# Crossbar transposes in place of TensorE transposes for q, k and the tails of a windowed attention and MLP kernel

## The chip, the cores and the metric

The kernel runs on one core of one Trainium2 chip. The metric is the device time of one execution in microseconds. The kernel before takes 324.83 us (median of 2 runs, 324.63 to 325.03). Engine names in the profile: PE is TensorE's matrix multiply, PEld its weight load, DVE is VectorE, ACT is ScalarE, POOL is GpSimd, SPq is SyncE's queue, from which nearly all DMA transfers of this kernel are issued.

## The reference, cut to what matters

```python
def _attn_ref(q, k, v):                       # each (8, 8, 576, 64): batch, head, position, head_dim
    scores = q @ k.T / sqrt(64)
    mask = (rel >= 0) & (rel < 64)            # rel = query position - key position
    attn = softmax(where(mask, scores, -1e9))
    return attn @ v

def reference(q, k, v, g_ln, w_ch1, w_ch2):
    x = attention, heads side by side: (8, 576, 512)
    xn = (x - mean) / sqrt(var + 1e-6) * g_ln
    return x + relu(xn @ w_ch1) @ w_ch2       # 512 -> 2048 -> 512
```

The inputs q and k are about 0.1 in size, so the scores are close to zero.

## The kernel before

The program works in groups. Group g runs the MLP of batch g (positions 0 to 511) and, between its steps, the attention of batch g+1 and the preparation of q, k and v of batch g+2. Positions 512 to 575 of all batches, the "tails", form a ninth group; tail i holds batches 2i and 2i+1. Each group from the second batch on has 30 slots: 16 first-layer blocks (slots 0 to 15) and 14 steps of the second layer, which uses 7 products in place of 8. `at(i, f, ...)` puts f into slot i. Every engine works through its own list in order (in the changed kernel PE stands idle for 7.17 us behind one wait, with all its later matmuls in the list).

q and k come from memory in float32, GpSimd casts them to float16, TensorE transposes them (the score matmul of this kernel takes them with the 64 elements of the head dimension on the partitions), and ScalarE copies the transposes from the accumulators (PSUM) to working memory (SBUF):

```python
def load_qk(b, half):                         # b >= 2: 4 heads a half, 4 rows to a partition: 1 KB runs
    nc.sync.dma_start(out=t..., in_=src[b, 4*half:4*half+4, 0:SM, :].rearrange("h (p j) d -> p h (j d)", j=4))

def t_main(b, x, half, eng=None):             # x = 0: q, x = 1: k
    for i in range(8):
        nc.tensor.transpose(out=tp[:, i, :], in_=src[:, i], identity=ident16)
    dst = qkT[b][x][:, 2*half:2*half+2, 64*x:64*x+512]
    evac(..., dst.rearrange("c h (p j) -> c h p j", j=j), tp...rearrange("c (h j) p -> c h p j", j=j))

def s_mm(g, j, ...):                          # 16 score matmuls of 64 x 128 keys and 64 queries
    ...
        lhsT = qkT[g][1][rows, hp, 64*w:64*w+128]
        rhs = qkT[g][0][rows, hp, 64*w:64*w+64]
        nc.tensor.matmul(out=sc[par][:, hp, iw, :], lhsT=lhsT, rhs=rhs, ...)
    ...
        nc.scalar.activation(out=pt[:, par], in_=sc[par], func=AF.Exp, bias=0.0, scale=scale)
```

Then VectorE multiplies `pt` by the mask, TensorE multiplies by v into `xps`, and VectorE writes the normalised attention into a tile of `x_norm`. That tile is later the residual input of the MLP, takes its sum, and is what is stored to memory.

```python
p_xn = tc.tile_pool(name="pxn", bufs=4)       # two tiles a batch: batch b+2 takes the tiles of batch b
def b_step(g, kb):
    ...
    nc.vector.tensor_tensor(out=xn, in0=xps[:, :, 0:D], in1=rcp_b, op=ALU.mult)
def store(kb):
    nc.sync.dma_start(out=out[g, 128*kb:128*kb+128, :], in_=x_norm[(g, kb // 2)][:, kb % 2, :])
```

So the store at the end of group g must have landed before the first `b_step` of batch g+2, which stands in slot 2 of the very next group. In the tail's cast the order will matter:

```python
def cast_tail(i):
    nc.gpsimd.memset(vt[:, :, :, D:D+1], 1.0) # vt has one buffer: waits for the tail before
    nc.gpsimd.tensor_copy(out=q16, in_=tq)
    nc.gpsimd.tensor_copy(out=k16, in_=tk)
    nc.gpsimd.tensor_copy(out=vt[:, :, :, 0:D], in_=tv)
```

The softmax here doesn't subtract the row's maximum and nothing guards it: scores larger than these inputs give would overflow.

## Time and profile before

| | kernel before |
|---|---|
| time | 324.83 us |
| profiled span | 322.6 us |
| PE busy | 309.6 us (96%) |
| ACT busy | 176.8 us (55%) |
| PE busy from 103 to 300 us | throughout |

The page of the kernel before: the busy time of each engine (with its share of the span and its number of instructions), then the granted clock of TensorE in 40 slices of the span (in tenths).

```profile
PE 309.6 (96%) x3229; PEld 204.6 (63%) x3229; DVE 204.3 (63%) x388; ACT 176.8 (55%) x292; POOL 164.6 (51%) x251
...
PEclk9999999999999999999999999999999999999998
```

PE is busy nearly all the time at full clock. The matmul time in the profile overlaps (each instruction's end is modelled), so what an instruction costs is read from start to start. The timeline of PE in the kernel before (start in us, duration, engine, line, operation, output and inputs, count), a block of 8 transposes and a block of 16 score matmuls with what follows each:

```profile
117.80 0.62 PE L216 MATMUL tp<-ident,qk 128*128 128x128 f16 x8
118.26 0.93 PE L435 MATMUL pB<-w2s,hrT 128*128 128x256 f16 x7
...
128.88 0.41 PE L263 MATMUL sc<-qkT,qkT 64*128 64x64 f16 x16
129.22 0.40 PE L232 MATMUL tpq<-ident,tq 128*128 128x128 f16 x4
```

Eight transposes take 118.26 - 117.80, about 0.45 us; the score block takes 0.34 us. SyncE's queue in the last part of the same group (the time of issue of each transfer, with the time that the issue took):

```profile
114.06 0.37 SPq L92 DMA_DIRECT2D qk<-in_q_dram  x1
115.05 0.37 SPq L92 DMA_DIRECT2D qk<-in_k_dram  x1
119.20 0.37 SPq L92 DMA_DIRECT2D qk<-in_q_dram  x1
120.19 0.37 SPq L92 DMA_DIRECT2D qk<-in_k_dram  x1
125.07 4.44 SPq L139 DMA_DIRECT2D v<-in_v_dram  x4
129.70 3.70 SPq L401 DMA_DIRECT2D out_dram<-xn  x4
```

The stores of the group are issued from 129.70 us. VectorE needs their tiles back at 135.47 us and waits 0.19 us there. So there is no slack at all, which one sees also in the group of that instruction in the page (after the last bar: idle time of the engine before it, and what ended it):

```profile
L297 DVE TENSOR_TENSOR xn<-xps,rcp 128x512 f32<-128x512 f32 x36 | 24.9, 692 | 3.3 <-DMA out_dram<-xn 2.2
```

The windows of the kernel before, over two stretches (busy time of each engine, then granted clock, busy share of the DMA engines and GB/s; the share can pass 1):

```profile
121.00:127.00 6.00, 6.00 (x67) 5.49 (x65) 2.23 (x5) 2.54 (x3) 5.77 (x11) 1.00 0.58 191
127.00:148.00 21.00, 21.00 (x261) 12.39 (x259) 14.92 (x28) 16.18 (x29) 11.27 (x18) 1.00 0.53 118
```

The DMA engines are half free here (0.58 and 0.53 busy).

### The profile page before, as it was taken

What the parts mean: (1) busy time and instruction counts of PE and PEld (TensorE: products, weight loads), DVE (VectorE), ACT (ScalarE), POOL (GpSimd) and SP (SyncE); (2) the same over time, 40 slices, a digit from 0 to 9 for tenths busy, and PEclk for the clock granted to TensorE, in tenths of its full rate; (3) what the DMA queues carried; (4) which work ended last, traced back from release to release, by engine and by line L of the source; (5) the groups of instructions that cost most, each with busy time, mean ns of one, the idle gap of its engine ahead of it and who ended that gap; (6) DMA issues with size and microseconds to landing.
All of it is one profiled execution on the core that took longest, in us unless ns stands there. A gap on an engine that the chain in (4) does not pass through costs nothing.

```text
span 322.6 us, 7813 instructions
## 1 busy us (share of the span) xinstructions
PE 309.6 (96%) x3229; PEld 204.6 (63%) x3229; DVE 204.3 (63%) x388; ACT 176.8 (55%) x292; POOL 164.6 (51%) x251
## 2 busy tenths in 40 slices
PE   7978999999989999999999999999999999999993
PEld 4556444687544578656964696459755865694582
DVE  0887764666885795489447954896559644751643
ACT  2576624487346754876457647775486157405600
POOL 7678765423991689079705982598036506200000
PEclk9999999999999999999999999999999999999998
DMA  8999999976089947904598459000570190003013
GB/s 194 282 385 259 363 306 295 264 267 133 35 276 227 207 139 204 241 2 133 173 259 183 132 168 259 26 2 2 171 182 2 24 241 33 0 2 131 0 36 98
DMA packets 85639, 51.08 MB, mean 158 GB/s; under 512 B 55682, under 2 KB 76674, under 8 KB 85603
## 3 DMA queue, kind: packets, MB, share of 16 engines
q1 hardware_dynamic: 84816, 48.11, 55.6%
q0 software_dynamic: 640, 2.33, 3.1%
q8 instruction: 25, 0.41, 0.5%
q10 hardware_dynamic: 146, 0.13, 0.1%
q14 instruction: 12, 0.09, 0.1%
HBM read 38.80 MB, written 9.44 MB: 150 GB/s over the span
## 4 chain that ended last, share of the span: by engine, by line
PE 85%; DVE 4%; SPq 3%; DMA 2%; POOL 2%; ACT 1%; issue 0%; ACTq 0%; POOLq 0%
PE hps L363 33%; PE pA L435 11%; PE pC L435 8%; PE pB L435 8%; PE hph L484 6%; PE ch L375 4%; PE xps L291 4%; PE tp L216 3%; PE sc L263 3%; DMA w1s<-in_moe_w_ch_dram 2%; PE ztp L328 2%; SPq L139 2%; POOL w1g L188 1%; PE ch L499 1%; DVE wT L532 1%; SPq L87 1%
## 5 line engine op out<-in xcount | busy, mean ns | idle before, releaser
L363 PE MATMUL hps<-zT,w1g 128*128 128x512 f16 x480 | 112.0, 379 | 0.0
L367 ACT ACTIVATE hrT<-hps 128x512 f16<-128x512 f32 x120 | 71.9, 599 | 35.1 <-PE hps L363 31.6
L363 PEld LDWEIGHTS <-w1g 128*128 128x128 f16 x480 | 44.1, 98 | 47.0 <-issue 1.0
L316 POOL TENSOR_SCALAR rsz<-mvg 128x1 f32<-128x1 f32 x28 | 12.2, 437 | 76.5 <-DVE mvg L302 75.5
L266 ACT ACTIVATE pt<-sc 128x512 f16<-128x512 f32 x72 | 39.0, 595 | 14.6 <-PE sc L263 13.1
L435 PEld LDWEIGHTS <-sS 128*128 128x128 f16 x448 | 43.0, 98 | 4.7
L207 ACT COPY qkT<-tp 128x1024 f16<-128x1024 f16 x26 | 26.2, 1012 | 33.6 <-PE tp L216 32.4
L126 POOL CAST qk<-qk 128x1024 f16<-128x1024 f32 x32 | 33.7, 1070 | 9.5 <-DMA qk<-in_q_dram 4.9
L442 DVE TENSOR_TENSOR xn<-pA,xn 128x512 f32<-128x512 f32 x28 | 19.2, 686 | 26.1 <-PE pA L435 17.4
L331 ACT COPY zT<-ztp 128x512 f16<-128x512 f16 x36 | 21.1, 586 | 26.5 <-PE ztp L328 26.1
L435 PEld LDWEIGHTS <-hrT 128*128 128x128 f16 x336 | 32.3, 98 | 5.0
L294 DVE RECIPROCAL rcp<-xps 128x8 f32<-128x8 f32 x36 | 7.4, 205 | 34.3 <-PE xps L291 34.1
L414 DVE TENSOR_TENSOR sS<-hrT 128x512 f16<-128x512 f16 (+1 forms) x42 | 21.4, 510 | 10.2 <-ACT hrT L367 10.2
L297 DVE TENSOR_TENSOR xn<-xps,rcp 128x512 f32<-128x512 f32 x36 | 24.9, 692 | 3.3 <-DMA out_dram<-xn 2.2
L435 PE MATMUL pA<-wT,sS 128*128 128x256 f16 x224 | 26.9, 273 | 0.0
L435 PE MATMUL pC<-w2s,sS 128*128 128x256 f16 x224 | 26.8, 273 | 0.0
L273 DVE TENSOR_TENSOR pt<-pt,mask 128x1024 f16<-128x1024 f16 x28 | 21.2, 762 | 8.6 <-ACT pt L266 8.5
L484 PE MATMUL hph<-zT,w1g 128*128 128x256 f16 x192 | 23.6, 273 | 2.5 <-ACT zT L331 1.1
L299 DVE BATCH_NORM_STATS2 stats<-xn 128x6 f32<-128x512 f32 x36 | 25.0, 695 | 1.2
L319 POOL TENSOR_SCALAR z<-xn,rsz 128x512 f16<-128x512 f32 x28 | 23.4, 836 | 2.9
L375 PE MATMUL ch<-w2s,hrT 128*128 128x512 f16 x96 | 23.7, 380 | 0.1
L484 PEld LDWEIGHTS <-w1g 128*128 128x128 f16 x192 | 18.0, 98 | 5.8 <-issue 2.2
(85 smaller groups left out, 437.2 us busy)
## 6 DMA issues: line engine op xcount, KB each, us to landing
out_dram<-xn SPq DMA_DIRECT2D x34, 256.0 KB, 3.6
qk<-in_q_dram SPq DMA_DIRECT2D x16, 512.0 KB, 4.8
qk<-in_k_dram SPq DMA_DIRECT2D x16, 512.0 KB, 5.9
v<-in_v_dram SPq DMA_DIRECT2D x32, 256.0 KB, 6.2
w2s<-in_moe_w_ch_dram SPq DMA_DIRECT2D x12, 512.0 KB, 5.6
w1s<-in_moe_w_ch_dram SPq DMA_DIRECT2D x4, 512.0 KB, 7.3
tk<-in_k_dram SPq DMA_DIRECT2D x8, 256.0 KB, 4.4
tv<-in_v_dram SPq DMA_DIRECT2D x8, 256.0 KB, 5.1
```

Of the source, the lines that this page charges most:

```text
L126: nc.gpsimd.tensor_copy(out=dst[:, :].rearrange("p (a j) e d -> p a e j d", j=j), in_=t[:, :].rearrange("p (a e j d) -> p a e j d", e=2, j ...
L207: nc.scalar.copy(out=out, in_=in_)
L266: nc.scalar.activation(out=pt[:, par], in_=sc[par], func=AF.Exp, bias=0.0, scale=scale)
L297: nc.vector.tensor_tensor(out=xn, in0=xps[:, :, 0:D], in1=rcp_b, op=ALU.mult)
L299: nc.vector.bn_stats(out=stats, in_=xv)
L319: nc.gpsimd.tensor_scalar(out=z, in0=xv, scalar1=rs, scalar2=nm, op0=ALU.mult, op1=ALU.add)
L363: nc.tensor.matmul(out=hps, lhsT=w1g[:, kc, 128 * hc:128 * (hc + 1)], rhs=zT[g][:, kc, :], start=(kc == 0), stop=(kc == NKC - 1),)
L367: nc.scalar.activation(out=hrT[:, hc, :], in_=hps, func=AF.Relu, bias=0.0, scale=1.0)
L375: nc.tensor.matmul(out=ch[kb], lhsT=hrT[:, hc, 128 * kb:128 * (kb + 1)], rhs=w2s[:, hc, :], start=(hc == 0), stop=(hc == NHC - 1),)
L414: nc.vector.tensor_tensor(out=o, in0=x, in1=y, op=op)
L435: nc.tensor.matmul(out=bank[which][:, p, :], lhsT=a[:, c, 128 * p:128 * p + 128], rhs=wv[:, c, :], start=(first and p == 0 and c == 0), st ...
L484: nc.tensor.matmul(out=hps[:, e], lhsT=w1g[:, kc, 128 * hc:128 * (hc + 1)], rhs=zT[g][:, kc, 256 * half:256 * half + 256], start=(kc == 0) ...
```

## The change

The intent is to take 176 transposes off TensorE, the busy engine, and 24 copies off ScalarE. For batches 4 to 7 the transposes of q and k, and those of all tails, become DMA transposes through the crossbar, issued from SyncE. q keeps its loads in 1 KB runs; its transposed columns then lie in another order, and the score matmul picks them with a step of 128 elements (256 bytes). k is loaded in 256-byte runs, so that its columns lie in order. The tails' casts and transposes move ahead of the v loads, and the first tail's steps in a group move to later slots. The casts now go into one tile for q and one for k, used by all batches in turn, and the tails' k shares the second of them. The core of the diff:

```diff
+    XQ = 4
+    cast16 = [p_const.tile([128, NHP, 4, 128], FP16, tag=f"cast16_{x}", ...) for x in range(2)]
 def load_qk(b, half):
+            elif b >= XQ and x == 1:
+                for c in range(2):
+                    s0 = 256 * half + 128 * c
+                    nc.sync.dma_start(out=t[:, 512*c:512*c+512].rearrange("p (h d) -> p h d", h=H),
+                                      in_=src[b, :, s0:s0 + 128, :].rearrange("h s d -> s h d"))
 def t_main(b, x, half, eng=None):
+        if b >= XQ:
+            if half == 0:
+                dst = flat(b, x)[:, 64 * x:64 * x + NHP * SM]
+                nc.sync.dma_start_transpose(out=dst.rearrange("p (a t) -> p a t", t=128),
+                                            in_=cast16[x][:, :, :, :].rearrange("p a c m -> p (a c m)"))
+            return
 def s_mm(g, j, ...):
+                    elif g >= XQ:
+                        c0 = SM * hp + 64 * (2 * j + iw)
+                        lhsT = flat(g, 1)[rows, c0:c0 + 128]
+                        qb = flat(g, 0)[rows, SM*hp + 16*(2*j+iw):SM*hp + 16*(2*j+iw) + 16]
+                        rhs = bass.AP(tensor=qb.tensor, offset=qb.offset, ap=[qb.ap[0], [1, 16], [128, 4]])
 ... (the same for the tails: two dma_start_transpose in t_tail) ...
-            ts = (10, 11, 14, 20) if n else (1, 2, 5, 11)
+            ts = (10, 11, 15, 20) if n else (5, 6, 10, 15)
-            for i, (x, half) in zip((17, 19, 21, 25), ...):
+            for i, (x, half) in zip((17, 17, 17, 17) if n >= XQ else (17, 19, 21, 25), ...):
                 at(i, t_main, n, x, half, 0)
                 at(17, load_qk, n + 1, 0)
                 at(18, load_qk, n + 1, 1)
-                at(23, load_v, n + 1, 0, 4)
+                at(24, load_v, n + 1, 0, 4)
-                at(24, cast_tail, i)
-                at(27, t_tail, i, 0)
-                at(29, t_tail, i, 1)
+                at(22, cast_tail, i)
+                at(22, t_tail, i, 0)
+                at(22, t_tail, i, 1)
```

More of the change, by code (lines that the diff above doesn't have):

```diff
@@ L41 @@
     EPS = 1e-6
+    XQ = 4
+    XZ = 99
     scale = 1.0 / (D ** 0.5)
@@ L77 @@
     qk32, qk16, v32 = {}, {}, {}
+    cast16 = [p_const.tile([128, NHP, 4, 128], FP16, tag=f"cast16_{x}", name=f"cast16_{x}") for x in range(2)]
     tail32, tail16, tailT, vT = {}, {}, {}, {}
@@ L90, in load_qk @@
                 )
+            elif b >= XQ and x == 1:
+                for c in range(2):
+                    s0 = 256 * half + 128 * c
+                    nc.sync.dma_start(
+                        out=t[:, 512 * c:512 * c + 512].rearrange("p (h d) -> p h d", h=H),
+                        in_=src[b, :, s0:s0 + 128, :].rearrange("h s d -> s h d"),
+                    )
             else:
@@ L110, in cast_tail @@
         q16 = p_in.tile([128, H, D], FP16, tag="tq16", name=f"tq16_{i}", bufs=1)
-        k16 = p_in.tile([128, 2, H, D], FP16, tag="qk16_1", name=f"tk16_{i}")
+        k16 = cast16[1][:, 0:2].rearrange("p r c (e d) -> p r (c e) d", d=D)
         vt = p_va.tile([128, 2, H, D + 1], FP16, tag="vt", name=f"vt_{i}", bufs=1)
@@ L122, in cast_qk @@
             t = qk32.pop((b, x, half))
-            dst = p_in.tile([128, 8, 2, D], FP16, tag=f"qk16_{x}", name=f"qk16_{x}_{b}_{half}")
+            if b >= XQ and x == 1:
+                nc.gpsimd.tensor_copy(
+                    out=cast16[x][:, :, 2 * half:2 * half + 2, :].rearrange("p a c m -> p c a m"),
+                    in_=t[:, :].rearrange("p (c a m) -> p c a m", c=2, a=NHP),
+                )
+                continue
+            dst = cast16[x][:, 2 * half:2 * half + 2, :, :].rearrange("p a c (e d) -> p (a c) e d", d=D)
             qk16[(b, x, half)] = dst
@@ L202, in alloc_qkT, with flat @@
         qkT[b] = [p_qkt.tile([128, NHP, SM + 64 * x], FP16, tag=f"qkT{x}", name=f"qkT{x}_{b}") for x in range(2)]
-        nc.gpsimd.memset(qkT[b][1][:, :, 0:64], 0.0)
+        if b < XQ:
+            nc.gpsimd.memset(qkT[b][1][:, :, 0:64], 0.0)
+        else:
+            nc.gpsimd.memset(qkT[b][1][:, 0, 0:64], 0.0)
+    def flat(b, x):
+        return qkT[b][x][:, :, :].rearrange("p h m -> p (h m)")
     def evac(x, out, in_):
@@ L229, in t_tail @@
                         p_qkt.tile([128, 2, NHP, 128], FP16, tag="tkT", name=f"tkT_{i}", bufs=1))
+            if XQ < B:
+                nc.sync.dma_start_transpose(out=tailT[i][0], in_=src[:, :, :].rearrange("p h d -> p (h d)"))
+                return
             tp = t_tile([128, NHP, 128], f"tpq_{i}")
@@ L233, in t_tail @@
         else:
+            if XQ < B:
+                nc.sync.dma_start_transpose(out=tailT[i][1][:, :, :, :].rearrange("p r h t -> p (r h) t"),
+                                            in_=src[:, :, :, :].rearrange("p r h d -> p (r h d)"))
+                return
             tp = t_tile([128, 2, NHP, 128], f"tpk_{i}")
@@ L258, in s_mm @@
                         rhs = tailT[j][0][rows, hp, 64 * iw:64 * iw + 64]
+                    elif g >= XQ:
+                        c0 = SM * hp + 64 * (2 * j + iw)
+                        lhsT = flat(g, 1)[rows, c0:c0 + 128]
+                        qb = flat(g, 0)[rows, SM * hp + 16 * (2 * j + iw):SM * hp + 16 * (2 * j + iw) + 16]
+                        rhs = bass.AP(tensor=qb.tensor, offset=qb.offset, ap=[qb.ap[0], [1, 16], [128, 4]])
                     else:
@@ L325, in zt_step @@
             zT[g] = p_grp.tile([128, NKC, 512], FP16, tag="zT" + sfx, name=f"zT_{g}", bufs=1 if sfx else 2)
+        if g >= XZ:
+            nc.sync.dma_start_transpose(out=zT[g][:, :, 128 * kb:128 * kb + 128], in_=z)
+            return
         ztp = t_tile([128, NKC, 128], f"ztp_{g}_{kb}")
@@ L745 @@
             at(21, make_vB, n)
-            for i, (x, half) in zip((17, 19, 21, 25), ((0, 0), (1, 0), (0, 1), (1, 1))):
+            for i, (x, half) in zip((17, 17, 17, 17) if n >= XQ else (17, 19, 21, 25),
+                                    ((0, 0), (1, 0), (0, 1), (1, 1))):
                 at(i, t_main, n, x, half, 0)
```

## The prediction

> **What bounds the kernel now.** TensorE. The busy table gives PE 309.6 of 322.6 us (96%), and the windows from 103 to 300 us show it busy throughout at full clock. From batch 2 on a group takes about 33 us (first-layer blocks start at 131.6, 165.1, 197.9, 231.2), and adding its pieces by start-to-start times in the timeline (64 first-layer matmuls at 0.221 us, 14 products at 0.875, attention, transposes) gives about 32.9: next to no slack. Only work taken off PE, or new PE waits, count.
>
> **Removed.** 176 PE transposes: 16 blocks of 8 for q and k of batches 4 to 7, and 4 tails of 4+8. A transpose's own duration (219 ns) misleads, because matmuls overlap. Start to start, a block of 8 takes 0.45 us (117.80 to 118.26), 56 ns each: 9.9 us, all on the critical path. ScalarE loses 24 evacuations, 22.6 us, but is not the limit: worth about nothing.
>
> **Added.**
> 1. 256 score matmuls read q with a 256-byte step. A score block of 16 takes 0.34 us now (128.88 to 129.22). [...] No trace of this case has such a read. Estimate: at twice the streaming time +0.1 us per block, 1.5 us over 16 blocks; at four times about 8 us.
> 2. 8 crossbar transposes of 512 KB and 8 tail ones, on SyncE's queue. [...] This trace has no transpose, but 512 KB loads land 4.8 to 5.9 us after issue. Batch 4's second cast ends at 120.2 us and its first scores start at 128.9, 127.1 once the blocks between are gone: k has 6.8 us from cast to use (batch 5: 7.2); q's transpose can start 1.1 us earlier. [...] expected 2 us in all.
> 3. k's loads of batches 4 to 7 become 256-byte runs, with some 20 us before their casts; no cost. Tail transposes have about 10 us, because their scores move from slot 1 to 5.
>
> **Sum.** 324.8 - 9.9 + 1.5 + 2 = 318.4; taken slightly lower because the slots look chosen to hide the transposes: **318.0 us, range 313.5 to 324.0**. Chances: faster by over 2% (under 318.3) 0.50, within 2% 0.43, slower 0.07.
>
> **What would show it.** PE's matmul count falls by 176; ScalarE's busy time falls by about 22 us to near 154. Groups that transpose batches 4 to 7 shorten by about 1.8 us each, those with tails by a further 0.67. Score blocks of batches 4 to 7 measure 0.34 to 0.45 us start to start, against 0.34 for batches 2 and 3. PE waits on transposes before a batch's first scores are 0 to 1 us each.
>
> **What would make it wrong.** Crossbar transposes far slower than a 512 KB load (over 4 us each): PE idles several us before each first score, and the whole gain goes. A strided read at four times or worse: score blocks of 0.8 us. Stores and v loads stuck behind a transpose in SyncE's in-order queue, so that casts or output buffers come late. With neither penalty nor lateness: about 315 us.

The sum is 324.8 - 9.9 + 1.5 + 2 = 318.4, taken to 318.0, its 2 us for late transposes about 0.5 us for each of batches 4 to 7. Its 1.5 us for the stepped read is the author's estimate, with assumed factors of two and four on what the trace shows: the 16 matmuls of a score block start in pairs 0.029 us apart (128.914, 128.943, 128.972), 0.23 us for eight pairs, and twice that is about 0.1 us more than the block's 0.34.

## The result, and the profile after

The changed kernel takes 367.74 us (median of 2 runs, 366.93 to 368.54): 1.132 times the kernel before (95% interval 1.121 to 1.143). Such ratios here are the mean time of one kernel's fast runs over that of the other's of the same rounds, so not quite the ratio of the medians. Executions over 1.5% slower than the fastest of the same kernel are left out of the means. The loss is 42.9 us, where a gain of 6.8 was predicted.

The page of the changed kernel, the lines that answer to those of before:

```profile
PE 319.6 (88%) x3053; PEld 205.6 (56%) x3053; DVE 205.0 (56%) x388; ACT 156.0 (43%) x268; POOL 163.2 (45%) x251
...
PEclk9999999999999999699996999779999999699998
```

PE has 176 matmuls fewer, as intended, and ACT lost 20.8 us. But PE's busy time rose by 10 us, its share fell to 88%, and the granted clock has dips that the kernel before has not. The timeline of PE in the changed kernel, the first score block of batch 4's second step, then the first stall, at the head of the next group (in brackets: idle time before the instruction, and its releaser):

```profile
135.27 1.05 PE L303 MATMUL sc<-qkT,qkT 64*128 64x64 f16 x16
136.25 2.76 PE L406 MATMUL hps<-zT,w1g 128*128 128x512 f16 x12
...
150.12 0.26 PE L331 MATMUL xps<-vB,pt 128*64 128x65 f16 x1 [7.17 <-DVE pt L313]
```

A score block with the stepped read takes 136.25 - 135.27 = 0.98 us instead of 0.34; all 16 such blocks take 0.98 to 0.99. And PE waits 7.17 us for the mask product of VectorE. The waits of the changed kernel, cut to those that matter (who waited for whom: us in total, times, longest):

```profile
DVE xn L337 <- DMA out_dram<-xn: 34.9, 3, 12.3
...
PE xps L331 <- DVE pt L313: 19.7, 3, 7.9
...
PE sc L303 <- DMA tkT<-cast: 9.4, 3, 5.4
...
PE sc L303 <- DMA qkT<-cast: 0.8, 2, 0.4
```

They read as a chain. VectorE must write the attention of batch 4 into an `x_norm` tile whose old contents (batch 2's result) are still waiting to be stored. It waits three times, 34.9 us in all. The mask product stands behind it in VectorE's list, and PE waits for that, 19.7 us. The transposes of q and k, which the prediction watched, make PE wait for only 0.8 us; those of the tails for 9.4 us. Why the stores are late shows in SyncE's queue at the same place as above:

```profile
120.90 5.05 SPq L237 DMA_TRANSPOSE qkT<-cast  x2
125.99 0.59 SPq L102 DMA_DIRECT2D qk<-in_q_dram  x1
126.63 2.40 SPq L97 DMA_DIRECT2D qk<-in_k_dram  x2
129.08 1.46 SPq L102 DMA_DIRECT2D qk<-in_q_dram  x1
130.58 3.99 SPq L97 DMA_DIRECT2D qk<-in_k_dram  x2
134.68 2.74 SPq L259 DMA_TRANSPOSE tqT<-tq  x1
137.51 1.25 SPq L266 DMA_TRANSPOSE tkT<-cast  x1
138.82 3.40 SPq L155 DMA_DIRECT2D v<-in_v_dram  x4
142.32 3.59 SPq L444 DMA_DIRECT2D out_dram<-xn  x4
```

The first store is issued at 142.32 us instead of 129.70. The next batch's first loads, which the kernel before issued at 114.06 and 115.05 us, are issued at 125.99 and 126.63: they stand behind the transposes, and the transposes had to wait for their casts (q's ends at 120.87 us). So the loads fall into the stretch just before the stores. Issues take longer too: 0.59 and 1.46 us for one of q's loads, 1.20 and 2.00 us for one of k's (means of two), where a load took 0.37; why, the profile does not show. The windows of the changed kernel over the same two stretches:

```profile
121.00:127.00 6.00, 6.00 (x60) 5.39 (x57) 3.40 (x7) 1.14 (x2) 5.12 (x9) 1.00 0.92 169
...
124.00:127.00 3.00, 3.00 (x32) 2.70 (x30) 0.79 (x2) 0.59 (x1) 3.00 (x5) 1.00 1.15 211
...
127.00:148.00 21.00, 13.84 (x131) 8.19 (x128) 4.41 (x8) 7.82 (x14) 3.91 (x7) 0.97 1.10 243
```

The DMA engines are now full from 122 us to the end of the second stretch (a busy share of 1.10 over the 26 us). In the first, almost nothing but the two crossbar transposes runs. Its 169 GB/s are a mean that takes in an empty first microsecond; once the transposes are under way (the line from 124 us) they move 211 GB/s with the engines full.

Last, the granted clock after a stall. Windows of the changed kernel across the second store stall (the first pair of numbers after the length is PE busy and matmuls, the clock stands third from the end):

```profile
192.00:194.00 2.00, 0.20 (x8) 0.20 (x10) 1.68 (x4) 0.00 (x0) 0.65 (x2) 0.50 1.04 230
194.00:196.00 2.00, 2.00 (x34) 1.38 (x31) 1.44 (x3) 0.53 (x2) 1.47 (x3) 0.50 1.19 209
196.00:198.00 2.00, 2.00 (x9) 0.97 (x8) 1.72 (x5) 1.26 (x4) 1.36 (x3) 0.50 1.22 209
198.00:200.00 2.00, 2.00 (x11) 0.88 (x10) 1.81 (x3) 1.24 (x3) 1.90 (x2) 0.97 0.08 13
```

PE restarts at 193.8 us and works at half clock until about 198. After the three store stalls (7.17, 7.86 and 4.63 us) and the two longer tail waits (2.35 and 5.39 us) PE works for 3.3 to 5.1 us at 0.50, worked out from such windows; after the tail wait of 1.70 us the clock stays full. Adding PE's busy time times (1 - clock) over the 2 us windows around these five waits gives 9.8 us of lost work. This is an upper figure: three score blocks with the stepped read lie in these stretches and take 0.98 us there too, as at full clock, so about 1.5 us of the 9.8 (an estimate, 3 times half of 0.98) was not lost.

So the places of the loss can be listed, all from this one profile and the one before. (z is the layer norm's result in float16, which GpSimd makes and TensorE transposes.)

| place on PE | us |
|---|---|
| transposes gone (176 at 56 ns, from before) | -9.9 |
| score blocks with the stepped read (16 blocks, 0.98 - 0.34 each) | +10.2 |
| waits behind the output stores | +19.7 |
| waits for the tails' transposes | +9.4 |
| waits for q's and k's transposes | +0.8 |
| half clock after stalls, at most | +9.8 |
| waits for z, 3.4 (GpSimd 2.8, VectorE 0.6) against 1.4 | +2.0 |
| sum | +42.0, measured +42.9 |

A list of places is not yet a list of causes: the experiments show that taking away a place does not give its time back.

### The profile page after: what moved, and what is told of

It reads as the page before. It is cut to its first block, busy times and chain, and to the rows that moved or that the text cites. A ratio compares the mean times of both kernels' runs of the same rounds, so it can differ in the third digit from the quotient of the medians.

```text
span 365.2 us, 7472 instructions
## 1 busy us (share of the span) xinstructions
PE 319.6 (88%) x3053; PEld 205.6 (56%) x3053; DVE 205.0 (56%) x388; ACT 156.0 (43%) x268; POOL 163.2 (45%) x251
## 4 chain that ended last, share of the span: by engine, by line
PE 52%; SPq 17%; DMA 14%; DVE 9%; POOL 4%; issue 3%; ACT 1%; POOLq 0%; DVEq 0%; ACTq 0%
PE hps L406 22%; PE pA L478 6%; SPq L155 5%; PE hph L527 4%; PE sc L303 4%; DMA qk<-in_q_dram 4%; SPq L97 3%; PE pC L478 3%; PE pB L478 3%; PE ch L418 3%; DMA w2s<-in_moe_w_ch_dram 3%; DMA out_dram<-xn 3%; PE xps L331 3%; SPq L102 3%; SPq L259 2%
## 5 line engine op out<-in xcount | busy, mean ns | idle before, releaser
L406 PE MATMUL hps<-zT,w1g 128*128 128x512 f16 x480 | 117.4, 395 | 0.0
L406 PEld LDWEIGHTS <-w1g 128*128 128x128 f16 x480 | 46.2, 101 | 54.4 <-issue 10.6
L356 POOL TENSOR_SCALAR rsz<-mvg 128x1 f32<-128x1 f32 x28 | 10.0, 358 | 114.8 <-DVE mvg L342 114.0
L337 DVE TENSOR_TENSOR xn<-xps,rcp 128x512 f32<-128x512 f32 x36 | 24.9, 692 | 36.1 <-DMA out_dram<-xn 34.9
L331 PE MATMUL xps<-vB,pt 128*64 128x65 f16 x256 | 15.1, 202 | 20.3 <-DVE pt L313 19.7
L331 PEld LDWEIGHTS <-pt 128*64 128x64 f16 x576 | 12.7, 114 | 33.0 <-DVE pt L313 21.2
L457 DVE TENSOR_TENSOR sS<-hrT 128x512 f16<-128x512 f16 (+1 forms) x42 | 24.2, 576 | 10.7 <-ACT hrT L410 10.7
L142 POOL CAST cast<-qk 128x1024 f16<-128x1024 f32 x24 | 25.3, 1058 | 9.2 <-DMA qk<-in_q_dram 5.0
L359 POOL TENSOR_SCALAR z<-xn,rsz 128x512 f16<-128x512 f32 x28 | 25.7, 918 | 2.9
L303 PE MATMUL sc<-qkT,qkT 64*128 64x64 f16 x512 | 23.3, 237 | 0.8 <-DMA qkT<-cast 0.8
```

Of the source, the lines that this page charges most:

```text
L142: nc.gpsimd.tensor_copy(out=dst[:, :].rearrange("p (a j) e d -> p a e j d", j=j), in_=t[:, :].rearrange("p (a e j d) -> p a e j d", e=2, j ...
L331: nc.tensor.matmul(out=xps[64 * r:64 * r + 64, h, :D + 1], lhsT=pt[:, par, hp, r, :], rhs=rhs, start=True, stop=True)
L359: nc.gpsimd.tensor_scalar(out=z, in0=xv, scalar1=rs, scalar2=nm, op0=ALU.mult, op1=ALU.add)
L406: nc.tensor.matmul(out=hps, lhsT=w1g[:, kc, 128 * hc:128 * (hc + 1)], rhs=zT[g][:, kc, :], start=(kc == 0), stop=(kc == NKC - 1),)
L457: nc.vector.tensor_tensor(out=o, in0=x, in1=y, op=op)
```

## The experiments

Theory A: the stores are late because of what was put ahead of them; the stepped read costs about 10 us by itself; the tails wait for their own reasons. Rivals: B, the DMA engines are full, so the queue's order does not matter; C, score blocks are slow because of DMA traffic or the clock, not the step; D, k's short runs and not the transposes fill the queue. All runs named here were compared with the kernel before on the same chip; 13 kernels ran, and every one passed the comparison with the reference. (A version with two more `x_norm` tiles was not run.)

**e1: stores issued by ScalarE.**

```diff
-            nc.sync.dma_start(out=out[g, 128*kb:128*kb+128, :], in_=x_norm...)
+            (nc.scalar if g > 1 else nc.sync).dma_start(out=out[g, 128*kb:128*kb+128, :], in_=x_norm...)
```

> The changed kernel, but the output stores of batches 2 to 7 are issued from ScalarE's queue instead of SyncE's. Theory A (order of issue): the three 12 us waits of VectorE on an output store come from the stores standing behind transposes and loads in SyncE's in-order queue; off that queue they vanish, TensorE gets back the 19.7 us that it idled for them and some of the slow clock after each, and the time falls by 20 to 28 us, to 340 to 348. The wait for output stores then totals under 5 us. Rival B (bandwidth): the 16 DMA engines are saturated at that point, so the stores land late wherever they are issued; the wait stays over 20 us in total and the time over 358.

Measured: 367.35 us, ratio 1.127 (1.124 to 1.131): no gain beside the 367.7 of the changed kernel. The waits of this run show why; ScalarE, in whose list the stores now stand, waits for transfers that have nothing to do with its own work, and PE waits for ScalarE:

```profile
PE hps L406 <- ACT hrT L410: 26.3, 6, 7.4
...
ACT hrT L410 <- DMA out_dram<-xn: 16.4, 2, 9.2
...
ACT hrT L410 <- DMA tqT<-tq: 13.3, 2, 7.5
```

VectorE's wait for stores is gone, as A said, but A's gain did not come. ScalarE's list now stands still around its stores: two of them take 3.60 us to issue from 129.40 us and two more 2.47 us from 137.46 us, and the exponential and the ReLU behind them start after 7.77 and 5.84 us of idle time, which the profile puts down to a load of k and to a tail's transpose. Where PE waited 19.7 us behind VectorE, it now waits 26.3 us behind ScalarE. The DMA engines are full here too (0.96 to 1.25 busy in windows of 3 us from 130 to 145 us), and a second issuing queue brought no gain (367.35 against 367.74). Whether the full DMA engines are what held the stores here, no run shows. The form of A that blamed SyncE's queue as such falls. What stands is: too much DMA work comes before the stores.

**e2: the loads of the next q and k behind the stores.**

```diff
-                at(17, load_qk, n + 1, 0)
-                at(18, load_qk, n + 1, 1)
+                at(30, load_qk, n + 1, 0)
+                at(30, load_qk, n + 1, 1)
```

> The changed kernel, stores on SyncE as they were, but the loads of the next batch's q and k are moved behind the stores of the group. Theory A: the stores are then issued about 9 us earlier (the six loads took 8.6 us of issue), the store waits fall to under 5 us in all, and the tail transposes, no longer behind those loads, come earlier too, so the 10.5 us of waits on the tail transposes fall to under 4 us: time 328 to 342. If the transposes themselves are what holds the queue, not the loads behind them, the store waits stay over 15 us in all and the time over 350.

Measured: 342.63 us (340.92 to 345.46), ratio 1.056 (1.050 to 1.061): 25.1 us less by the medians, with the same transfers, only later. The line of the stores in this run's waits:

```profile
DVE xn L337 <- DMA out_dram<-xn: 14.6, 3, 6.2
```

The time is just outside A's range (328 to 342), and the store waits stay higher than expected (14.6 against under 5), so the transposes and v loads that still stand ahead of the stores matter as well. B falls in the form in which order would not matter. Of the three waits of PE for tail transposes one is left, the last tail's, 5.7 us.

**e3: the stepped read alone, in the kernel before** (wrong scores).

```diff
+                        if 4 <= g:
+                            qf = qkT[g][0][:, :, :].rearrange("p h m -> p (h m)")
+                            qb = qf[rows, SM*hp + 16*w:SM*hp + 16*w + 16]
+                            rhs = bass.AP(..., ap=[qb.ap[0], [1, 16], [128, 4]])
```

> Wrong result on purpose: the kernel before, with nothing but the 256-byte step in q's read by the score matmuls of batches 4 to 7 (same bytes count, wrong elements). Theory A: the stride alone makes a score block 0.98 us instead of 0.34, 16 blocks, 10.2 us: 334 to 336 us. Rival C: score blocks are slow in the changed kernel because DMA traffic of the transposes shares the memory, or because of the lower clock; then here the block stays under 0.5 us and the time under 328.

Measured: 335.19 us (334.97 to 335.26) against 325.05: +10.1 us, as expected. The timeline of this run:

```profile
166.07 1.05 PE L267 MATMUL sc<-qkT,qkT 64*128 64x64 f16 x16
167.06 1.92 PE L439 MATMUL pC<-w2s,sS 128*128 128x256 f16 x16
```

The block takes 0.99 us with no transpose in the program and full clock. C falls; the step alone eats the whole intended gain.

**e4: q read in runs of 16, and put in order by the exponential** (right result). The matmul's output columns may come in any order, as long as somebody restores it; ScalarE reads the scores anyway.

```diff
-                        rhs = bass.AP(..., ap=[qb.ap[0], [1, 16], [128, 4]])
+                        rhs = bass.AP(..., ap=[qb.ap[0], [128, 4], [1, 16]])
+            # batches 4 to 7:
+                nc.scalar.activation(out=pt[:, par].rearrange("p h w (t j) -> p (h w) t j", j=4),
+                                     in_=sc[par][:, :].rearrange("p h w (j t) -> p (h w) t j", j=4), ...)
```

> The changed kernel, right result: the score matmul reads q in four runs of 16 neighbouring elements, so scores come out in permuted columns, and ScalarE's exponential puts them back in order by reading PSUM with a step. Theory A: score blocks fall from 0.98 to 0.34 to 0.45 us and the time by 8 to 11 us, to 357 to 360, the exponentials stay at 0.6 to 0.7 us, the store waits stay. If any access that is not one run costs as much, the block stays near 0.98 us and the time is unchanged.

Measured: 366.55 us (363.25 to 367.51), ratio 1.127: about 1 us less, not 8 to 11. The mechanism worked: the score block is back at 0.34 us (159.73 to 160.07 in this run), and the exponential takes the same 0.60 us with or without the stepped read of PSUM (595 and 596 ns in e8, which has both). But the waits grew:

```profile
DVE xn L342 <- DMA out_dram<-xn: 39.8, 3, 14.2
...
PE sc L303 <- DMA tkT<-cast: 14.4, 3, 5.4
```

They were 34.9 and 9.4. PE gets to the same barrier earlier and waits there longer: in the changed kernel the chain of waits runs through DMA, not through PE. The expectation missed this, because it added places as if they were causes.

**e5: k in 1 KB runs** (k's columns out of order).

```diff
-            elif b >= XQ and x == 1:
+            elif False:
```

> Wrong values on purpose: the changed kernel, but k of batches 4 to 7 is loaded in 1 KB runs like q (one transfer of 512 KB per half instead of two of 256 KB in 256-byte runs); casts, transposes, stride and order are unchanged. Theory A2: the stores are late because of the sum of work put ahead of them, of which the short runs of k are a part of 3 to 4 us per group and the transposes the larger part of 6 to 8 us; then the store waits fall from 34.9 to 22 to 28 us and the time to 353 to 362. Rival D (k's runs are the cause, not the transposes): the waits fall under 10 us and the time under 345. Rival E (k's runs cost nothing): unchanged within 3 us.

Measured: 362.49 us, ratio 1.115 (1.111 to 1.118): 5.3 us less than the changed kernel. The store waits fall from 34.9 to 28.5 us. Just outside the range given (353 to 362, waits 22 to 28), but D and E fall: the way k is loaded is a real but small part of the delay. The edit halves the number of k's issues too (one transfer of 512 KB in place of two of 256 KB); so it does not show whether the short runs or the number of transfers cost the time. Of the waits for tail transposes it leaves one, 5.4 us. Whether the transposes are the larger part, as A2 says, this run does not show; e2 and e8 say that it is the sum of all that stands ahead.

**e6: e2 and e4 together.**

> Next batch's q and k loads behind the stores (as in e2) and q read in runs of 16 (as in e4), result right. In e4 alone the 10.2 us that TensorE saved were eaten by longer waits for DMA, as the chain of waits there ran through the DMA queue. If that is so, with the queue relieved most of the 10.2 us must show: e2's 342.6 falls to 332 to 336. If the runs are worth nothing in themselves, the time stays within 2 us of 342.6.

Measured: 339.10 us (336.88 to 339.30), 3.5 us below e2 and not 7 to 11. The queue was not relieved enough: the store waits of this run are 15.7 us, the last tail's 5.7 us. Still a miss.

**e7: a tail's q and k cast ahead of its v tile.**

```diff
-        nc.gpsimd.memset(vt[:, :, :, D:D + 1], 1.0)
         nc.gpsimd.tensor_copy(out=q16, in_=tq)
         nc.gpsimd.tensor_copy(out=k16, in_=tk)
+        nc.gpsimd.memset(vt[:, :, :, D:D + 1], 1.0)
```

> The changed kernel; only cast_tail is reordered, so that q and k of a tail are cast before the memset of the v tile, which waits for the previous tail's attention. In the changed kernel the last tail's scores stand in the same slot as, and right behind, the attention step of the tail before, which frees that v tile; so its casts and transposes start only then, and TensorE waits 5.4 us for them near 309 us. Theory: that wait goes (under 1 us) and the time falls by 4 to 7 us, with the shorter slow-clock stretch after it, to 360 to 364. Rival: the transposes are late because of the loads ahead of them in the queue; the wait stays over 4 us.

Measured: 361.88 us, ratio 1.114 (1.110 to 1.117): 5.9 us less than the changed kernel, as expected. The waits for tail transposes fall from 9.4 us in three places to 3.7 us in two; the longest, 5.4 us, is gone. That one was made by the new slots: the last tail's scores stood in the slot of the step that frees its v tile.

**e8: all mends, v loads behind the stores too** (right result). e6 and e7 together, and:

```diff
-                at(24, load_v, n + 1, 0, 4)
+                at(30, load_v, n + 1, 0, 4)
```

> All mends together, result right: q, k and v loads of the next batch behind the stores, q in runs of 16, tail casts ahead of the v tile. Theory: with the stride gone, and nothing but transposes ahead of the stores, the gain of 9.9 us on TensorE shows apart from rests of waits of 0 to 6 us: 315 to 322, faster than the kernel before. If the transposes still hold the stores back by themselves (bandwidth), store waits stay over 10 us and the time over 328.

Measured: 325.07 us, with a wide spread (320.91 to 327.14; of the 6 runs two count as slow), ratio of the fast runs 0.994 (0.989 to 0.999). Over all six the mean is 324.4 us, against 325.2 before. The profiled run took 322.05 us. The big waits are gone in it: the stores are issued from 131.23 us, 0.6 us is waited in all behind them, no dip of the clock, and on PE these waits are the largest that remain after the start:

```profile
PE ztp L376 <- POOL z L364: 4.7, 4, 1.4
...
PE sc L303 <- DMA qkT<-cast: 1.9, 3, 0.8
```

So the loss is won back, but of the hoped-for 9.9 us of gain only 0.6% of the time, about 2 us, is kept by the fast runs and less by all six, and the expected range was missed. The transposes of q, k and tails still stand ahead of the stores, and these now wait 0.6 us: the transposes alone are not too much, it takes the loads behind them as well.

**e9 and e10: fewer batches through the crossbar.** e8 with `XQ = 7` (batch 7 and tails) and `XQ = 6`; q and k loads are moved only where the batch of the group goes through the crossbar.

```diff
-    XQ = 4
+    XQ = 7            # e10: 6
+                late = n >= XQ
+                at(30 if late else 17, load_qk, n + 1, 0)
+                at(30 if late else 18, load_qk, n + 1, 1)
+                at(30 if late or TAILS.get(g + 1) else 23, load_v, n + 1, 0, 4)
```

> Right result: the mends of e8, but only batch 7 and the tails go through the crossbar; batches 4 to 6 keep TensorE's transposes and 1 KB loads of k, and no q or k load of a next batch is moved. Batch 7 is prepared in a group that loads nothing for a next batch. Theory: TensorE loses 32 + 48 transposes at 56 ns, 4.5 us, and no store, scores or z step waits: 320 to 321.5, a smaller gain than the 9.9 us of all, but kept, and with a narrower spread than e8's (320.9 to 327.1). If the tail transposes in the queue hold up stores or loads by themselves, the time stays over 323.

> As e9 with batch 6 through the crossbar too (its group loads batch 7's q and k, which are then put behind the stores): TensorE loses 6.3 us. Theory: 318.5 to 321, if the later loads of batch 7 do not delay GpSimd's casts and z steps; if they do, as in e8, 1 to 2 us of it come back and the time equals e9's within 1.5 us.

Measured: e9 324.70 us, ratio 0.999 (0.997 to 1.001); e10 323.01 us (322.66 to 323.21), ratio 0.994 (0.992 to 0.996). Both miss their ranges by 2 to 3 us. (In both, the v loads go behind the stores also where the next group has tails.) In both, PE waits for z more than in the kernel before (3.8 and 4.5 us, in e8 4.7, before 1.4); the new waits, up to 1.4 us each, lie in the three groups that work on tails. Those groups have the moved tail slots; a run with the moved slots alone was not made. e10 has the tight spread that e8 lacks.

**e11: the stepped read in pairs, in the kernel before** (wrong order).

```diff
-                            rhs = bass.AP(..., ap=[qb.ap[0], [1, 16], [128, 4]])
+                            rhs = bass.AP(..., ap=[qb.ap[0], [2, 8], [128, 4], [1, 2]])
```

> Wrong order on purpose: the kernel before, with q read by the score matmuls of batches 4 to 7 in pairs of neighbouring elements (4 bytes) with steps of 256 bytes between pairs, where e3 had single elements. [...] If so, the score block is back near 0.34 us and the time at 325 to 327. If the cost goes by the number of jumps, half of e3's 10.1 us remains: about 330, blocks of 0.6 to 0.7 us.

The sentence before "If so" is cut, because no trace or run shows it; the first case is that pairs take the cost of the step away.

Measured: 329.02 us against 324.59, ratio 1.012 (1.010 to 1.014); the score block takes 0.56 us:

```profile
165.27 0.62 PE L267 MATMUL sc<-qkT,qkT 64*128 64x64 f16 x16
165.83 1.92 PE L439 MATMUL pC<-w2s,sS 128*128 128x256 f16 x16
```

The result lies between the two expectations, nearer the second. Two neighbours in a row take away two thirds of the cost of a block (0.64 us becomes 0.22) and a little over half of the time (10.1 us becomes 4.4; by the ratio, 3.1 to 4.7). Runs of 16 (e4) take away all of a block's cost.

**e12 and e13: the first cast of a group behind the z step.** e8 and e10 with

```diff
-            at(11, cast_qk, g + 2, 0)
+            at(13, cast_qk, g + 2, 0)
```

> e8 with the first half of the next batch's q and k cast in slot 13 instead of 11, that is behind the z step of slot 12 on GpSimd. In e8 TensorE waits 4.7 us for z in four places, the three long ones (1.4 us) in the groups that carry a tail, whose z step the change moved from slot 5 to slot 10, right in front of that cast. If this crowding of GpSimd is what eats the rest, the waits for z fall under 1.5 us and the time by 2 to 4 us against e8's fast runs, to 317 to 321. If the rest comes from loads that land late, the waits move to GpSimd's casts and the transposes, and the time stays at e8's 321 to 327 with its spread.

> e10 (batches 6, 7 and tails through the crossbar) with the same move of the cast. By the same theory e10's 4.5 us of waits for z fall under 2 us and the time goes from 323.0 to 320 to 321.5, with the narrow spread that e10 has; unchanged within 0.7 us if the cast's slot does not matter.

Measured: e12 323.02 us (322.06 to 328.70, the last of these counted as slow), ratio 0.993 (0.991 to 0.995); e13 325.95 us, ratio 1.005 (1.001 to 1.008), slower than e10. In e12 the waits for z stay at 5.0 us, and those for the transposes of q and k grow from 1.9 to 3.6; in e13 PE now waits 2.2 us for casts, too, and 1.5 us behind a store again. The theory that this cast is what crowds GpSimd falls. Where the rest of the 9.9 us goes is only partly settled: in e8's profile about 4 us are new waits for z (GpSimd 4.7 and VectorE 0.6, before 1.4) and 2 us waits for transposes. GpSimd waits 1.8 us there for transposes out of the shared cast tile (0.6 in the changed kernel), which was not tested by itself. The rest is not explained.

## Why the prediction was wrong

Point by point:

- *What bounds the kernel now.* Right: e3 adds 10.1 us of PE work and the time rises by 10.1 us.
- *Removed.* Right in its size as far as the runs show: 176 matmuls and 20.8 us of ScalarE are gone. e8's profiled span is 2.3 us shorter than before and holds about 6 us of waits for z and for transposes that the kernel before has not, so about 8 of the 9.9 us are accounted for.
- *Added 1, the stepped read.* That the step costs time was right, and the term was mis-sized: "+0.1 us per block, 1.5 us over 16 blocks" measured 0.64 us a block and 10.1 us (e3). The line beside it, "at four times about 8 us", was the nearer one. This alone cancels the gain.
- *Added 2, the transposes.* The prediction asked when their data are needed, and put 2 us in the sum for coming late. That was near: 0.8 us of waits in all. The step that failed is the sum: "expected 2 us in all" counted only the reader of the transposes. What stands behind them in the queue was left to the last paragraph ("Stores and v loads stuck behind a transpose ...") and got no price. It cost 19.7 us of waits, and about 6.5 of the at most 9.8 us lost to the slow clock (the windows after the three store stalls). The trace of before held what was needed: loads issued from 114.06 us, stores from 129.70, their tiles needed at 135.47 and already 0.19 us late. Behind the transposes the first loads came 11.9 us later (125.99) and the first store 12.6 us later (142.32), and the stores had no microsecond to give.
- *Added 3.* "k's loads of batches 4 to 7 become 256-byte runs ... no cost" failed: e5 gives 5.3 us back. The casts had their 20 us, but the stores that stand behind these loads had not. "Tail transposes have about 10 us" failed for all but one tail: 9.4 us of waits, of which 5.4 us because the moved slots put the last tail's scores right behind the step that frees its v tile (e7), and the others because their transposes queue behind the loads (e2 removes them, and so does e5).
- *Sum.* 318.0 us predicted, 367.74 measured. Of the ways named to go wrong, two came true, the stepped read and the stores behind the queue; the first named, transposes so slow that PE idles several us before each first score, did not: they land 5.8 us after issue, q's loads in the same kernel 6.1. But they hold the DMA engines longer than loads of the same size (211 GB/s with the engines full, changed kernel, 124 to 127 us, against 332 GB/s for loads in 1 KB runs with the engines 95% busy, kernel before, 121 to 124 us), and it was the queue and not the reader that paid for it.

The mended kernels show that the change can be had without its loss, for 0.6 to 0.7% (e8, e10, e12). e10 is the firmest of the three: all its runs are fast and lie within 0.6 us. What keeps the rest of the gain stays open. One simple order was not tried: the next batch's loads ahead of the transposes, where the first of them stood before.

## What to carry to other kernels

When work moves from a busy engine to a DMA queue, do not ask only when its own data are needed: list everything that stands behind it in that queue, with the slack of each, and pay for the smallest. The five longer stalls of the matrix engine here (2.35 us and more) were charged twice, once as idle time and once as half clock for 3.3 to 5.1 us after them. And where a stepped read is needed, try it on another engine: here the exponential read the scores with a step at no cost (0.60 us either way), while the matmul's operand paid threefold (0.98 us against 0.34).
